# An attention and two-layer feed-forward kernel: fills for TensorE's early waits, the counts' transfer first, a last round by tile, and a new step order

## The chip, the cores and the metric

The kernel runs on one core of one Trainium2 chip. The metric is the device time of an execution in microseconds (us). Three executions of the kernel before took 528.06, 528.44 and 529.01 us; the median is 528.44.

## The reference

All values are 32-bit on the chip (inputs may come as 64-bit words). For 2 batches of 768 tokens, with 8 heads of 64:

```
scores = q k^T / 8, plus -slope(head) * distance; kept where the key is one of the
         first n_global, or among the n_local up to the query's own
x      = softmax(scores) v                          (1536 tokens x 512)
h      = x w_in (512 x 1024);  y = layernorm(h * softmax(h)) * g;  x2 = y w_out (1024 x 512)
g2     = prelu(x2 w_in2, alpha)  (512 x 2048);      out = g2 w_out2 (2048 x 512)
```

## The kernel before, in words

**Tiles.** The 1536 tokens are 12 tiles of 128. For tile i the first stage does: scores (`s{i}`, two steps of eight products, L653), bias and maximum on VectorE (`ttr`, L674), exponentials on ScalarE (`exp`, L686), sums (`sum`, L697), normalising on GpSimd (`norm`, L704), transposes on TensorE into the two `pt` buffers (`pp`, L711), their copies (`ptc`), products with v (`xp`, L732), and a split of the result into a high and a low part (`xh`, `xl`). Then four projection steps (`hp{i}.0` to `hp{i}.3`, L767), each of six 512-wide products with `w_in`, the softmax and normalisation of h, transposes (`yt`, L833), and, for each pair of tiles, the product with `w_out` (`f`, L868). Every large product is made of three: high by high, high by low, low by high.

**Weights.** They arrive as 64-bit words. VectorE decodes a 512-wide unit in three passes (L909, L915, L922), ScalarE casts the high part (L941) and GpSimd subtracts it for the low part (L947). `w_in` has eight units, `w_out` eight. A projection step `hp{i}.c` needs units 2c and 2c+1.

**Second layer.** From about 240 us on, for each batch and each of 16 slices f of the 2048 columns: two products `h` (L1004), the prelu on VectorE, ScalarE and GpSimd (`p`, `q`, `gh`, `gl`), and six steps `o{b}.{f}.{t}`, one for each of six tiles t, that add slice f into tile t's accumulator (L1046). After f = 15 each tile is copied out of the accumulator (`ev`) and stored (`out`); the very last tile goes in two halves.

**Who sets the order.** All of this is a list of steps (`p.op`) with costs, needs, buffers and a due time: a base for each tile plus constants in `PRI` plus a table `ADJ` by step and tile. `Plan.order` (L135) walks it with a cost model: it takes the engine and step that can start first, and among those that can start at once the one with the smallest due time; TensorE stays with its kind of step (fp32r products, transposes, attention products, scores) if one is due within `window`. The steps are then written out by hand in that order; each engine runs its own in order. Three rules of the model matter here. A step's result is ready `DRAIN` + `LAT` after its end, which is 0.22 + 0.05 us behind a TensorE step. TensorE's costs double for 3.5 us after the start and after an idle time of over 2 us. And 30 filler steps (`warm`, L1096) of two transposes of the identity each have due time 1000 and up, so that they go where nothing else can start at once: 15 write the projection's accumulator, 15, after `s2.0`, the accumulator of `xp`.

**Ahead of the plan.** The counts n_global and n_local are loaded on SyncE's queue (L1312); VectorE makes distances from them and a flag that says whether the fast plan applies; every engine loads the flag into a register (L1341) and branches (L1348). Loads written ahead of the branch: the first `w_in` unit on ScalarE's queue (L1320), tile 0's two halves of queries and keys on SyncE's (L1323), two small vectors on ScalarE's, and four more `w_in` units on SyncE's (L1346), written behind the flag's load. What stands outside the plan is ordered by the framework.

```
            if e == "PE":
                if s - free[e] > 2.0:
                    cold = s + 3.5
...
                if s < cold:
                    c *= 2
...
            for j in succ[k]:
                need[j] -= 1
                ready_at[j] = max(ready_at[j], end + (self.LAT if e != "Z" else 0.0))
```

Of the kernel before, what the change touches and what calls it, by code (L numbers as in the profile page):

```python
# [16 lines left out]
P = 128  # L17
B, H, S, D = 2, 8, 768, 64
# [19 lines left out]
    "fb": [12.1, 25.5, -36.9, 15.6, -51.3, -38.9], "window": 40.6, "warm": 30,  # L38
# [10 lines left out]
    "bias": [-14.38, -0.57, -13.62, -36.09, -9.24, 3.17, 79.56, 27.81],  # L49
    "biaso": [-35.88, -34.51, 29.02, -45.8, 12.27, 5.79, 12.9, -39.68],  # L50
    "biase": [11.25, -16.84, -13.23, -15.82, -6.36, -33.05, -25.07, 2.78],
    "lv": [-1.11, -35.58, -25.57, -93.69, -40.77, -64.76, -5.42, -4.44, 16.09, 40.62, 15.31, -13.09],
    "s": [76.17, 48.99, -1.79, -6.29, 18.91, -35.34, -3.19, 1.82, 4.29, 5.11, 37.66, -32.16],
    "ttr": [17.97, 14.68, 9.26, -0.75, 24.27, 1.35, -15.44, 44.7, 38.08, 44.52, 77.23, 18.58],
    "exp": [99.95, 17.84, 75.5, 70.15, 68.93, 21.61, 105.36, 54, 36.83, 49.25, 25.14, 20.37],
    "sum": [65.68, 7.88, 17.67, -22.02, 14.99, 23.4, 68.37, 13.75, 33.79, 44.17, 14.09, 30.57],
    "norm": [-28.87, -32.62, 6.09, -65.61, -51.55, -113.76, -7.63, -51.34, -8.17, -14.02, -57.42, -42.13],
    "pp": [42, 3.18, 9.24, 15.23, 22.4, -52.81, -19.62, 8.44, -19.69, 7.5, -63.78, -27.87],
    "ptc": [31.98, 24.29, 16.59, 13.26, -19.88, 27.62, 55.76, 15.29, 29.15, 39.13, 56.39, 31.43],
# [4 lines left out]
    "wild": [-16.78, -71.31, -22.06, -78.1, -76.78, -74.65, -91.3, -78.16],  # L64
    "wi": [5.84, -7.23, 8.63, 14.11, 39.89, 27.88, 6.37, 30.66],
    "wold": [3.18, -27.83, 0.2, -42.59, -4.05, -51.23, -59.18, -139.63],
# [9 lines left out]
    "wld": [-60.46, 30.51, -6.9, -43.59, -6, -39.28, -71.17, -74.53, -40.67, -27, -26.6, -59.42, -94.56,  # L76
        -71.11, -58.44, -37.12],
    "w": [-6.92, -18.15, -3.62, -19.12, 7.9, -25.84, -46.69, -31.5, 17.04, -9.48, -0.07, 24.34, 23.84, 37.97,
        26.01, 29.91],
    "xsh": [-36.5, -104.9, -69.33, 0.49],  # L80
    "xsl": [-18.31, 12.23, 178.41, 14.34],
    "h": [-0.45, -22.06, -6.71, -25.99, -26.69, -13.38, -21.23, -5.88, -9.22, -36, 7.14, -11.38, -44.05,
        -19.53, -8.32, 9.67, -1.41, -20.25, -27.94, -26.27, -8.77, 13.58, -6.42, -6.67, 5.95, -8.6, 7.18, 4.35,
        -5.24, -5.24, 6.81, -23.86],
    "pre": [47, 15.26, 20.19, 1.09, 5.66, 4.51, 1.73, -56.3, -1.61, -12.93, -24.13, -2.19, -11.64, -7.5,
        -12.94, -11.02, 15.1, -13.05, 1.61, -12.3, -8.69, -9.72, -27.94, -3.94, -30.83, -32.43, -3.34, -7.57,
        -38.89, -39.41, -24.55, -18],
    "o": [25.13, 15.32, 1.71, 16.18, 13.48, 5.18, 9.35, -10.38, 23.35, 48.62, 54.94, 17.03, 51.65, 48.18,
        61.52, 65.49, 53.89, 52.56, 42.95, 51.04, 74.74, 72.62, 64.17, 78.16, 98.8, 63.21, 109.55, 136.07,
        93.51, 111.81, 113.4, 98.74],  # L90
# [10 lines left out]


class Plan:


    LAT = 0.05
    SWITCH = {"r": 0.03, "tr": 0.07, "xp": 0.11, "sp": 0.12}
    DRAIN = {"PE": 0.22, "DVE": 0.09, "ACT": 0.1, "POOL": 0.05}

    def __init__(self, window=2.5):  # L110
        self.ops, self.by_name, self.size = [], {}, {}
        self.window = window

# [21 lines left out]
    def order(self, free):  # L135
# [37 lines left out]
        while done < n:  # L173
# [26 lines left out]
            if e == "PE":  # L200
                if s - free[e] > 2.0:
                    cold = s + 3.5
# [3 lines left out]
                if s < cold:  # L206
                    c *= 2
# [1224 lines left out]
```

## Time and profile before

| what | value |
|---|---|
| median of three executions | 528.44 us |
| the profiled execution: its own time | 528.57 us |
| its span, first to last instruction | 526.8 us |
| TensorE (PE) busy | 504.1 us, 96% |
| VectorE (DVE) busy | 312.5 us, 59% |
| ScalarE (ACT) busy | 202.0 us, 38% |
| GpSimd (POOL) busy | 200.1 us, 38% |
| mean granted clock of TensorE | 0.985 |

The profile is one execution. Times count from the first instruction. PE is TensorE's products (a transpose is one of them), PEld its weight loads, SP is SyncE; a q behind an engine is its sequencer or its DMA queue. L and a number is a line of the kernel. A busy engine may be a slow one: the granted clock of TensorE is given in tenths in the page's slices (forty of 13.2 us each) and as a share in a table of stretches.

### The profile page before, as it was taken

How to read it: one execution, taken by the hardware profiler on the slowest of the kernel's cores; microseconds unless marked ns; L12 is line 12 of the kernel's file. 1: busy time of each engine (PE TensorE's matmuls, PEld its weight loads, DVE VectorE, ACT ScalarE, POOL GpSimd, SP SyncE). 2: the span in 40 equal slices, each digit the busy share in tenths (PEclk: the TensorE clock that was granted, in tenths of full speed). 3: DMA queues.
4: the chain of work that ended last, by engine and by line, in shares of the span. 5: the costliest groups of instructions: out<-in, count | busy, mean ns of one | idle time of the engine just before them, and what ended most of it. 6: DMA issues, size and time to landing. Idle time of an engine off the chain costs nothing.

```text
span 526.8 us, 8161 instructions
## 1 busy us (share of the span) xinstructions
PE 504.1 (96%) x3084; PEld 439.4 (83%) x3084; DVE 312.5 (59%) x671; ACT 202.0 (38%) x488; POOL 200.1 (38%) x205
## 2 busy tenths in 40 slices
PE   3599999999999999999999999999999999999995
PEld 3366778888889789899998998999888899889884
DVE  4979898374443658549976878988622423213130
ACT  4757875374354687334223222232311201101112
POOL 2667776023030338023316566554611412213230
PEclk9779999999999999999999999999999999999999
DMA  6965563132130210202333234340002100000003
GB/s 207 369 216 169 171 212 119 51 100 72 31 101 2 70 42 1 81 0 82 116 125 105 96 119 121 119 126 35 1 1 81 40 1 1 1 0 1 0 2 126
DMA packets 14959, 43.61 MB, mean 83 GB/s; under 512 B 1984, under 2 KB 3264, under 8 KB 14912
## 3 DMA queue, kind: packets, MB, share of 16 engines
q1 hardware_dynamic: 14336, 42.34, 25.3%
q10 hardware_dynamic: 576, 0.67, 0.5%
q8 instruction: 26, 0.43, 0.3%
q14 instruction: 21, 0.17, 0.1%
HBM read 39.86 MB, written 3.15 MB: 82 GB/s over the span
## 4 chain that ended last, share of the span: by engine, by line
PE 90%; DVE 4%; ACT 2%; DMA 1%; issue 1%; POOL 1%; POOLq 0%; DVEq 0%; ACTq 0%
PE m L774 12%; PE m L502 9%; PE m L503 9%; PE m L504 9%; PE h L503 9%; PE h L504 9%; PE h L502 8%; PE x L737 4%; PE s L659 4%; PE pt L716 4%; PE pt L503 3%; PE pt L504 3%; PE pt L502 3%; PE pt L838 2%; PE x L503 1%; PE x L504 1%
## 5 line engine op out<-in xcount | busy, mean ns | idle before, releaser
L1040 POOL TENSOR_TENSOR gl<-t,gh 128x384 fp32r<-128x384 f32 x64 | 70.7, 1107 | 129.5 <-ACT gh L1033 126.5
L1020 DVE TENSOR_SCALAR t<-h,a_sb 128x384 f32<-128x384 f32 x64 | 39.4, 616 | 96.6 <-POOL gl L1040 64.6
L1033 ACT CAST gh<-t 128x384 fp32r<-128x384 f32 x64 | 32.6, 513 | 144.0 <-PE pt L503 77.1
L502 PE MATMUL h<-x2h,w2h 128*128 128x384 f32 x192 | 64.5, 336 | 0.0
L503 PE MATMUL h<-x2l,w2h 128*128 128x384 f32 x192 | 64.5, 336 | 0.0
L504 PE MATMUL h<-x2h,w2l 128*128 128x384 f32 x192 | 64.5, 336 | 0.0
L704 POOL TENSOR_TENSOR pr<-pr,sm 128x512 f32<-128x512 f32 (+1 forms) x48 | 47.3, 1012 | 32.6 <-DVE sm L698 23.4
L502 PE MATMUL m<-lh,woh 128*128 128x256 f32 x192 | 55.8, 290 | 0.0
L503 PE MATMUL m<-ll,woh 128*128 128x256 f32 x192 | 54.2, 282 | 0.0
L504 PE MATMUL m<-lh,wol 128*128 128x256 f32 x192 | 54.2, 282 | 0.0
L686 ACT ACTIVATE pr<-lg,nmx 128x256 f32<-128x256 f32 (+1 forms) x96 | 46.4, 486 | 10.8 <-DVE nmx L674 10.7
L502 PEld LDWEIGHTS m<-lh,woh 128*128 128x128 f32 x192 | 36.4, 190 | 3.8 <-issue 1.5
L947 POOL TENSOR_TENSOR w2l<-wf,w2h 128x512 fp32r<-128x512 f32 x21 | 29.2, 1392 | 26.5 <-ACT w2h L941 26.5
L503 PEld LDWEIGHTS m<-ll,woh 128*128 128x128 f32 x192 | 36.6, 190 | 1.2
L502 PEld LDWEIGHTS h<-x2h,w2h 128*128 128x128 f32 x192 | 36.1, 188 | 1.8
L503 PEld LDWEIGHTS h<-x2l,w2h 128*128 128x128 f32 x192 | 36.0, 188 | 1.8
L816 POOL TENSOR_TENSOR st<-st,mhalf 128x1 f32<-128x1 f32 x12 | 6.6, 549 | 80.7 <-DVE st L811 80.6
L915 DVE SCALAR_TENSOR_TENSOR wf<-wr,wf 128x512 int32<-128x512 int32 x32 | 36.8, 1149 | 0.4
L504 PEld LDWEIGHTS m<-lh,wol 128*128 128x128 f32 x192 | 36.6, 191 | 0.0
L1027 DVE SCALAR_TENSOR_TENSOR t<-h,t 128x384 f32<-128x384 f32 x64 | 35.4, 553 | 1.2
L504 PEld LDWEIGHTS h<-x2h,w2l 128*128 128x128 f32 x192 | 36.0, 188 | 0.0
L774 PE MATMUL m<-wih,xh 128*128 128x512 f32 x96 | 33.6, 431 | 0.7 <-ACT xh L748 0.7
(160 smaller groups left out, 1159.1 us busy)
## 6 DMA issues: line engine op xcount, KB each, us to landing
wr<-in_w_out SPq DMA_DIRECT2D x24, 512.0 KB, 3.6
wr<-in_w_in SPq DMA_DIRECT2D x16, 512.0 KB, 3.5
qk<-in_kq SPq DMA_DIRECT2D x20, 384.0 KB, 4.1
v<-in_vw SPq DMA_DIRECT2D x10, 512.0 KB, 3.7
x<-in_w_in SPq DMA_DIRECT2D x7, 512.0 KB, 6.9
out<-x SPq DMA_DIRECT2D x11, 256.0 KB, 2.1
x<-in_w_in ACTq DMA_DIRECT2D x1, 512.0 KB, 6.3
wr<-in_kq SPq DMA_DIRECT2D x2, 256.0 KB, 6.9
```

The source lines that it names most:

```text
L502: nc.tensor.matmul(o, sh, mh, start=first, stop=False)
L503: nc.tensor.matmul(o, sh, ml, start=False, stop=False)
L504: nc.tensor.matmul(o, sl, mh, start=False, stop=last)
L686: nc.scalar.activation(pr[:, j, :n], self.tiles["lg", i, h][:, :n], AF.Exp, bias=self.tiles["nmx", i, hf][:, hl : hl + 1], scale=-1.0, acc ...
L704: nc.gpsimd.tensor_tensor(pr[:, :, :n], pr[:, :, :n], r.unsqueeze(2).to_broadcast([P, 2, n]), ALU.mult)
L774: nc.tensor.matmul(hp[:, ns], st[:, c, :], mv[:, c, ns], start=f, stop=l)
L915: nc.vector.scalar_tensor_tensor(m["m"], self.tiles["wraw", name][:, :, 1], -0x40000000, m["m"], ALU.bitwise_and, ALU.bitwise_or)
L947: self.eng(e).tensor_tensor(lo, src(), f32(hi), ALU.subtract)
L1020: nc.vector.tensor_scalar(t, o(), 0.0, self.a_sb[:, f : f + 1], ALU.min, ALU.mult)
L1027: nc.vector.scalar_tensor_tensor(t, o(), 0.0, t, ALU.max, ALU.add)
L1033: nc.scalar.copy(gh, self.tiles["t", b, f, n])
L1040: nc.gpsimd.tensor_tensor(gl, self.tiles["t", b, f, n], f32(self.tiles["gh", b, f, n]), ALU.subtract)
```

## The change

- The 30 `warm` steps go. Instead, ahead of a scores, `pp`, `xp`, `yt` or first projection step, `idle()` writes as many transposes of the identity as the planner's own idle time before that step holds: (idle - 0.2) / 0.11, for steps that start before 60 us of its clock and waits over 0.35 us. Until the first projection step is placed they write the projection's accumulator; after it, the step's own output, and then only the wait after that output is free is counted.
- 24 transposes of the identity are written ahead of the branch, behind the flag's load.
- The first `w_in` unit is loaded on SyncE's queue behind the first half of tile 0's queries and keys; beside the counts' transfer only the two small ones are issued first.
- In the model a TensorE step may follow a TensorE step that it needs at once, and costs no longer double.
- In the last batch a tile's step for f = 14 waits for the tile before to have had f = 15.
- Some buffer releases and first uses name all tiles instead of the last one or two.
- `window` and every number of `ADJ` are new (cut here).

```diff
@@ -35,7 +35,7 @@
 YN_ACT = 1
 PRI = {
     "hpb": [-22.7, -30.5, -41.3, -50.8, -5.7, 15.7, -32.6, 6.6, 14.8, -15.7, -2.9, 22.1],
-    "fb": [12.1, 25.5, -36.9, 15.6, -51.3, -38.9], "window": 40.6, "warm": 30,
+    "fb": [12.1, 25.5, -36.9, 15.6, -51.3, -38.9], "window": 119.5, "warm": 30,
     "base": [-80.5, -35.1, -9.2, -5.2, 15.5, 19.1, 66.6, 102.8, 108.9, 162.8, 180.8, 178.6], "bias0": 11.1,
     "biaso": 4.0, "biase": 39.9, "load": 13.1, "s": 13.0, "sum": -26.6, "norm": 50.1, "pp": -26.4,
     "ptc": -0.2, "xp": -4.8, "xh": -42.6, "hp": -3.1, "ln": 30.3, "yt": 46.9, "f": 45.8, "x2c": 55.8,
@@ -46,48 +46,47 @@
 }
 START = {"PE": 6.0, "DVE": 6.2, "ACT": 6.1, "POOL": 6.45, "SP": 6.1, "Z": 6.0, "DMA": 14.0}
 ADJ = {
...
 }
 SCALE = 0.125
 
@@ -104,6 +103,7 @@
 
 
     LAT = 0.05
+    FILL = 60.0
     SWITCH = {"r": 0.03, "tr": 0.07, "xp": 0.11, "sp": 0.12}
     DRAIN = {"PE": 0.22, "DVE": 0.09, "ACT": 0.1, "POOL": 0.05}
 
@@ -154,7 +154,9 @@
         free = dict(free)
         dma = free.pop("DMA", 0.0)
         cand = {k for k in range(n) if need[k] == 0}
-        done, last, res, shared, cold = 0, None, [], 0.0, free["PE"] + 3.5
+        done, last, res, shared = 0, None, [], 0.0
+        self.fill = {}
+        res_hp = [None]
 
         def slot_time(o):
             r = 0.0
@@ -198,13 +200,15 @@
             o = ops[k]
             cand.discard(k)
             if e == "PE":
-                if s - free[e] > 2.0:
-                    cold = s + 3.5
+                early = res_hp[0] is None
+                idle = s - (free[e] if early else max(free[e], slot_time(o)))
+                if o[0].startswith("hp"):
+                    res_hp[0] = s
+                if s < self.FILL and idle > 0.35:
+                    self.fill[o[0]] = int((idle - 0.2) / 0.11), early
                 if o[6] != last and last is not None:
                     s += self.SWITCH[o[6]] + 0.2 * (last == "sp")
                 last = o[6]
-                if s < cold:
-                    c *= 2
             if o[9] and e == "DVE":
                 c += max(0.0, free["POOL"] - s)
                 shared = s + c
@@ -229,7 +233,8 @@
                     released[u[0]][place[u]] = freed[u]
             for j in succ[k]:
                 need[j] -= 1
-                ready_at[j] = max(ready_at[j], end + (self.LAT if e != "Z" else 0.0))
+                same = e == "PE" and "PE" in ops[j][1]
+                ready_at[j] = max(ready_at[j], free[e] if same else end + (self.LAT if e != "Z" else 0.0))
                 if need[j] == 0:
                     cand.add(j)
             res.append((s, free[e], e, k))
@@ -593,6 +598,12 @@
             else:
                 nc.vector.tensor_copy(dst, xp[:, : 2 * P])
 
+    def idle(self, o):
+
+        count, early = self.fill
+        for _ in range(count):
+            self.nc.tensor.transpose(self.hp[:, :P] if early else o, self.ident, self.ident)
+
     def eng(self, e):
         return {"DVE": self.nc.vector, "ACT": self.nc.scalar, "POOL": self.nc.gpsimd}[e]
 
@@ -653,6 +664,7 @@
         for hf in range(2):
             rawslot = ("raw", (i, hf)) if i else ("wr", ("r", hf))
             def emit(e, hf=hf):
+                self.idle(self.sq[0][:, :P])
                 for j in range(2):
                     for pj in range(2):
                         w = self.tiles["qk", i, hf][pj * D : (pj + 1) * D, j]
@@ -711,6 +723,7 @@
             def emit(e, pair=pair):
                 pr = self.tiles["pr", i, pair]
                 pp = self.tiles["pp", i, pair] = self.next_pt()
+                self.idle(pp[:, :P])
                 for j in range(2):
                     for c in range(nch):
                         nc.tensor.transpose(
@@ -731,6 +744,7 @@
 
             def emit(e, pair=pair):
                 pt, vs = self.tiles["pt", i, pair], self.vs[i]
+                self.idle(self.xp[:, pair * P : (pair + 1) * P])
                 for c in range(nch):
                     for j in range(2):
                         h = pair * 2 + j
@@ -766,6 +780,8 @@
         for c in range(NC):
             def emit(e, c=c):
                 xh, xl = self.tiles["xh", i], self.tiles["xl", i]
+                if c == 0:
+                    self.idle(hp[:, :P])
                 for st, mv, f, l in (
                     (xh, self.wih, c == 0, False), (xh, self.wil, False, False), (xl, self.wih, False, c == NC - 1)
                 ):
@@ -833,6 +849,7 @@
         for q in range(2):
             def emit(e, q=q):
                 pp = self.tiles["yt", i, q] = self.next_pt()
+                self.idle(pp[:, :P])
                 for c in range(4):
                     f = q * 4 + c
                     nc.tensor.transpose(pp[:, c * P : (c + 1) * P], y()[:, f * P : (f + 1) * P], self.ident)
@@ -994,8 +1011,8 @@
                     p.op(f"xsl{b}.{n}.{c}", None, {"DVE": 0.5, "POOL": 1.03}, b0 + PRI["xs"] + 0.1 * c, emit, port=True,
                          after=[f"xsh{b}.{n}.{c}"], uses=[(f"x2s{n}", b)])
             accs = [self.hp[:, 0:512], self.hp[:, 512:1024], *self.pts, self.xp, self.m2]
-            ln = f"{self.last}"
-            first = [[f"sq{ln}"], [f"sq{ln}"], ["cl_pt"], ["cl_pt"], [f"xl{ln}"], [f"xc{self.last_pair}.{NC - 1}"]]
+            sq, xl, xc = ([f"{s}{i}{x}" for i in range(k)] for s, x, k in (("sq", "", 12), ("xl", "", 12), ("xc", ".3", 6)))
+            first = [sq, sq, ["cl_pt"], ["cl_pt"], xl, xc]
             for f in range(NF2):
                 fb = b0 + f * PRI["m2f"]
                 for n in range(2):
@@ -1052,6 +1069,8 @@
                     dep = [f"gl{b}.{f}.{t // 3}", f"w{f}.1lo", f"o{b}.{f - 1}.{t}"]
                     if f == 0:
                         dep += first[t] if b == 0 else []
+                    if b == B - 1 and f == NF2 - 2 and t > 0:
+                        dep.append(f"o{b}.{NF2 - 1}.{t - 1}")
                     g = ("gh", (b, f, t // 3)), ("gl", (b, f, t // 3))
                     pri = fb + PRI["o"] + (0.5 * t if not tail else 3 * t - (NF2 - 1 - f) * PRI["m2f"] + 8)
                     p.op(f"o{b}.{f}.{t}", "PE", 0.69, pri, emit, after=dep, uses=[(f"acc{t}", b), *g], kind="r")
@@ -1093,15 +1112,6 @@
         self.plan_bias(p, ats)
         for i in range(n):
             self.plan_attn(p, i, r0, ats, at)
-        for k in range(PRI["warm"]):
-            early = k < PRI["warm"] // 2
-
-            def emit(e, o=self.hp if early else self.xp):
-                for c in range(2):
-                    nc.tensor.transpose(o[:, c * P : (c + 1) * P], self.ident, self.ident)
-
-            p.op(f"warm{k}", "PE", 0.22, 1000.0 + k, emit, kind="tr", after=[] if early else ["s2.0"],
-                 uses=[] if early else [("x", f"warm{k}")])
         units = [(c, h) for c in range(NC) for h in range(DF // DM)]
         for u, (c, h) in enumerate(units):
             cs = slice(h * DM, (h + 1) * DM)
@@ -1141,11 +1151,11 @@
             self.open_pool("hp2", pools, space=bass.MemoryType.PSUM)
             pools["hps"] = [pools["hp2"].tile([P, 512], F32, name=f"h2{k}") for k in range(2)]
 
-        p.op("cl_s", "Z", 0.0, 0, close_s, after=[f"ttr{last}.{h}" for h in range(H)])
-        p.op("cl_ats", "Z", 0.0, 0, close(["ats"], "m2", "w2c"), after=[f"exp{i}.{h}" for i in seq[-2:] for h in range(H)])
+        p.op("cl_s", "Z", 0.0, 0, close_s, after=[f"ttr{i}.{h}" for i in seq for h in range(H)])
+        p.op("cl_ats", "Z", 0.0, 0, close(["ats"], "m2", "w2c"), after=[f"exp{i}.{h}" for i in seq for h in range(H)])
         p.op("cl_at", "Z", 0.0, 0, close(["at"], "w2a"), after=["cl_ats", f"hp{last}.{NC - 1}"])
         p.op("cl_wo", "Z", 0.0, 0, close(["wo", "m1"], "w2b"), after=["cl_at", f"f{self.last_pair}.{NC - 1}.1"])
-        p.op("cl_pt", "Z", 0.0, 0, None, after=[f"ll{last}.{q}" for q in range(2)])
+        p.op("cl_pt", "Z", 0.0, 0, None, after=[f"ll{i}.{q}" for i in seq for q in range(2)])
         self.plan_moe2(p, pools)
         return p
 
@@ -1176,6 +1186,7 @@
         with self.tc.manual_schedule():
             for name, e, emit in p.order(START):
                 if emit is not None:
+                    self.fill = p.fill.get(name, (0, False))
                     emit(e)
         for name in ("w2b", "w2a", "w2c", "m2", "hp2"):
             self.pool_cms.pop(name).__exit__(None, None, None)
@@ -1317,10 +1328,11 @@
     em.w_in_alloc(cpool)
     r0 = []
     wl = []
-    wl.append(em.w_in_raw[0](nc.scalar.dma_start))
     for hf in range(2):
         r = wring.tile([P, 2 * DM], F32, "wr", "r0")
         r0.append(em.load_raw(0, hf, r))
+        if hf == 0:
+            wl.append(em.w_in_raw[0]())
     nc.scalar.dma_start(em.g_sb, em.g_ln)
     nc.scalar.dma_start(em.a_sb, em.alpha)
     with tc.high_priority():
@@ -1343,8 +1355,11 @@
     ps = ctx.enter_context(tc.tile_pool(name="ps", bufs=1, space=bass.MemoryType.PSUM))
     em.psum_pools(ps)
 
+    wm = em.ps_m1("wm")[:, :P]
     while len(wl) < len(wring.bufs["wx"]):
         wl.append(em.w_in_raw[len(wl)]())
+    for _ in range(24):
+        nc.tensor.transpose(wm, em.ident, em.ident)
     with tc.If(rv > 0) as cmp:
         em.fast_phase(wring, nw, r0, wl)
     with cmp.Else():
```

## Rows read from the trace of the kernel before

**Rows 1.** The page: busy time of the engines, the clock by slices, the chain's shares.

```profile
PE 504.1 (96%) x3084; PEld 439.4 (83%) x3084; DVE 312.5 (59%) x671; ACT 202.0 (38%) x488; POOL 200.1 (38%) x205
...
PEclk9779999999999999999999999999999999999999
...
PE 90%; DVE 4%; ACT 2%; DMA 1%; issue 1%; POOL 1%; POOLq 0%; DVEq 0%; ACTq 0%
```

**Rows 2.** Stretches: length, busy us by engine, granted clock, DMA share, GB/s.

```profile
8.40:34.40 26.00, 19.04 (x98) 14.25 (x98) 23.13 (x69) 17.78 (x61) 11.90 (x15) 0.74 0.86 308
...
19.60:24.00 4.40, 1.38 (x5) 0.50 1.02 411
...
34.40:80.00 45.60, 44.30 (x331) 32.38 (x330) 41.36 (x117) 35.89 (x94) 35.07 (x34) 1.00 0.60 185
...
520.30:526.80 6.50, 1.08 (x8) 0.85 (x8) 0.42 (x1) 0.37 (x1) 0.00 (x0) 0.85 0.55 185
34.40:520.30 485.90, 483.93 (x2980) 424.30 (x2979) 286.97 (x593) 182.31 (x424) 185.95 (x171) 1.00 0.22 68
```

**Rows 3.** The chain, steps at the full clock: start, us, engine, tile, line.

```profile
41.44 1.02 PE x L737 x16
...
44.07 1.06 PE s L659 x8
45.13 1.60 PE m L774 x6
...
82.31 1.39 PE m L774 x6
...
90.20 0.87 PE pt L716 x8
```

**Rows 4.** TensorE's waits: who for whom, us in total, times, longest.

```profile
PE s L659 <- DMA qk<-in_kq: 3.2, 1, 3.2
```

**Rows 5.** The chain's first transfer; SyncE's queue in the timeline, 5 to 9.3 us.

```profile
0.74 5.53 DMA ni<-in_n
...
8.38 1.29 SPq L445 DMA_DIRECT2D x<-in_w_in  x3
```

**Rows 6.** DMA issues of the last stores: KB each, us from issue to landing.

```profile
out<-x SPq DMA_DIRECT2D x1, 256.0 KB, 2.0
...
out<-x ACTq DMA_DIRECT2D x1, 128.0 KB, 4.6
```

**Rows 7.** The fillers' line in three stretches: ns min/median/max, first and last start; a stretch.

```profile
L1101 PE MATMUL m<-ident x6: 421/421/421, 10.2 to 11.3; 128*128 128x128 f32 x6
...
L1101 PE MATMUL m<-ident x11: 272/273/273, 13.2 to 14.3; 128*128 128x128 f32 x11
...
60.00:300.00 240.00, 1.58 (x10) 1.18 (x10) 1.00 0.27 80
```

**Rows 8.** The chain, 24 to 29.3 us; then VectorE in the timeline, idle time in brackets.

```profile
24.04 1.08 PE pt L716 x4
25.13 1.48 PE x L737 x12
26.61 2.01 PE s L659 x8
28.62 0.65 PE x L737 x4
...
28.76 0.42 DVE L674 CUSTOM_DVE_ANT_0 lg<-s,biaso 128x256 f32<-128x256 f32 x1 [1.47 <-PE s L659]
...
35.60 0.42 DVE L674 CUSTOM_DVE_ANT_0 lg<-s,biase 128x256 f32<-128x256 f32 x1 [1.11 <-PE s L659]
```

**Rows 9.** VectorE by line, 8 to 26 us: the second of a unit's three passes.

```profile
L915 DVE SCALAR_TENSOR_TENSOR m<-x,m 128x512 int32<-128x512 int32 x6 | 4.1, 690 | 0.0
```

**Rows 10.** The end: a stretch, and the last activations on GpSimd.

```profile
519.00:523.00 4.00, 2.38 (x14) 1.60 (x12) 0.42 (x1) 1.52 (x3) 0.00 (x0) 1.00 0.99 361
...
512.58 1.01 POOL L1040 TENSOR_TENSOR gl<-t,gh 128x384 fp32r<-128x384 f32 x1 [1.04 <-ACT gh L1033]
```

More of the change, by code (lines that the diff above doesn't have):

```diff
@@ L48 @@
 ADJ = {
[L49 to L59, printed above, removed]
[4 rows of a table removed]
-    "wild": [-16.78, -71.31, -22.06, -78.1, -76.78, -74.65, -91.3, -78.16],
@@ L65 @@
-    "wi": [5.84, -7.23, 8.63, 14.11, 39.89, 27.88, 6.37, 30.66],
-    "wold": [3.18, -27.83, 0.2, -42.59, -4.05, -51.23, -59.18, -139.63],
[9 rows of a table removed]
[L76 to L87, printed above, removed]
@@ L88 @@
-    "o": [25.13, 15.32, 1.71, 16.18, 13.48, 5.18, 9.35, -10.38, 23.35, 48.62, 54.94, 17.03, 51.65, 48.18,
-        61.52, 65.49, 53.89, 52.56, 42.95, 51.04, 74.74, 72.62, 64.17, 78.16, 98.8, 63.21, 109.55, 136.07,
-        93.51, 111.81, 113.4, 98.74],
+    "bias": [-15, 218.7, 220.4, 84.5, 30.2, 251.7, 462.2, 330.9],
+    "biaso": [69.1, -90.2, 98.2, -102.4, -52.3, 100.5, 205.3, 34.2],
+    "biase": [-256.7, -21.5, -21.5, 46.2, 14, 198.7, -71.8, 154.5],
+    "lv": [146.5, 31.6, -130.7, 105.3, 137.9, -212.2, -21.3, 57.1, 203.2, 112.7, 85.4, 30.9],
@@ new lines @@
+    "s": [256.9, 191.8, -103.6, 381.8, 156.7, -1.6, 28.3, 175.1, 148.7, 195.7, 150.9, -64.4],
+    "ttr": [136.5, -100.5, -256.8, -133.5, -27.5, -86.1, -120, 228.4, 93.8, 96.6, 195.2, 81.6],
+    "exp": [278.1, 153.5, -17.3, 174.1, 303, 117.2, 50.2, 225.6, 271, 53.2, -229.9, -71.8],
+    "sum": [62.8, 208, -84, 95.5, 286.5, -62.6, 248.2, 211.2, 228.9, 236.7, 25.9, 142.7],
+    "norm": [4.9, -1.9, -132.9, -34.2, -55.5, -333.8, 17.9, -253.3, -218.8, 9.6, -362.3, -451],
+    "pp": [80.5, -12.1, 12.6, 116.2, 413, 88.1, 33.3, 99, 177.2, 57.5, -215, 9.2],
@@ new lines @@
+    "ptc": [57.9, 63.5, 28.9, 224.8, 86.9, 45.3, -27.7, 214.6, 163.5, 137.5, 74.9, 178.8],
[4 rows of a table added]
+    "wild": [216.3, 52.5, -35.2, -73, 76, 86, -15.4, 364.6],
+    "wi": [101.8, 49.2, 81.8, 32.1, 265.5, 65.2, 99.6, 272.1],
+    "wold": [194.8, -15.5, -69.2, -24, -319.6, 242.6, -120.9, -418.7],
[9 rows of a table added]
+    "wld": [-194.8, 19.5, -45.8, -49, -16.1, 52.7, -255.2, -112.5, -57.5, -0.2, 47.5, -85.2, -125, -89.4, 51.3,
+        -179.2],
+    "w": [-92.5, 29, 7, 109.9, 239.2, -34.6, 28, 70.2, 203.5, 191.5, 159.9, 375.9, 223, 253, 230.1, 433.6],
@@ new lines @@
+    "xsh": [-120, -7.6, -301.3, 292.2],
+    "xsl": [225.2, 219.5, 905, 128.9],
+    "h": [131.8, 295.5, 173.7, 161.8, 99.7, 254, 205.4, 240.3, 143.8, 174.2, 340.3, 154.3, 204.1, 204, 304.7,
+        274, 247.5, 133.2, 214.8, 172.9, 111.5, 222.8, 244.1, 132.7, 210.9, 154.6, 205, 293.6, 203.3, 178.7,
+        312.8, 205.2],
+    "pre": [-69.4, -77.4, -102.6, -41.7, -133.8, -86.8, -165.3, -230.1, -156.4, -178.2, -200.3, -145.8, -126,
+        -116.7, -193.6, -173.2, -50.6, -229.7, -281.8, -285.5, -242.4, -122.5, -178.1, -125.3, -315.4, -172.9,
+        -199.9, -221.3, -284.5, -257.7, -200.8, -227.6],
@@ L91 @@
+    "o": [1.6, -51.6, 31.9, 68.6, 46.2, -52.7, 8.2, 6.6, 126.8, 142.7, 204, 49.5, 168.4, 189.3, 200.1, 220.5,
+        144.1, 115.4, 238.1, 225.8, 170.6, 168.3, 121.2, 175, 263.8, 152.3, 129.9, 337, 147.9, 323.3, 215.7,
+        153.9],
 }
```

26 rows, old and new, of the table ADJ are left out of this document.

## The prediction, made before the result was known

> **What bounds the kernel now.** I read the page first: TensorE is busy 96% of the span and is 90% of the chain that ended last [rows 1]. So a change pays only where TensorE idles, runs slowly, or does work that isn't needed. The clock digits are low in the second and third slice alone [rows 1]. Then I cut the span by stage [rows 2]. From 34.4 to 520.3 us TensorE is busy 483.9 of 485.9 us: that stretch has 2.0 us to give, plus whatever is removed from it. [...] Before 8.4 us TensorE does nothing, and after 520.3 nothing that the output needs; the span ends 6.5 us later.
>
> How much of the 26.0 us up to 34.4 is needed? At the full clock the work done there would take: scores of tile 1, 2 x 1.06, and of tile 0, half as wide, some 2 x 0.6; eight transposes 0.87; sixteen attention products 1.02; two of tile 0's four projection steps 2 x 1.39 [rows 3]. Sum 8.0. So the start wastes 18.0 us on top of the first 8.4. These, the 6.5 us at the end, the 2.0 us of idle time and the dummies already there are all that can be had; the rest, some 490 us, is work.
>
> What holds the start? The longest wait of TensorE behind the first scores is 3.2 us, for tile 1's queries [rows 4]. In front of them stands the transfer of the two counts, 0.74 to 6.27 us, from which VectorE works out the flag; the flag also holds SyncE, whose next three weight loads go out only at 8.38 [rows 5]. VectorE itself is busy 23.1 of the 26.0 us, and 41.4 of the next 45.6 [rows 2]: it is nearly the bound of the start.
>
> **The change, part by part.** The sum is made against the profiled execution: its own time 528.57, of which 526.8 is the span; the 1.8 us around it stay. The median, 528.44, is 0.13 below.
>
> *Counts first.* A 512 KB load that went out together with the counts moves from ScalarE's queue to SyncE's, behind the first half of tile 0's queries. The counts (2 KB) took 5.5 us [rows 5]; a 256 KB store with nothing beside it took 2.0 [rows 6]. The gain lies between 0 and 3.5; I take 1.7, the middle, as other loads still follow at once. It moves flag, branch, bias tables and the held loads alike. The moved load comes 256 KB later in its queue, some 0.7 us at the 361 GB/s of a full stretch [rows 10]; the bias tables give VectorE work until then.
>
> *Warm clock.* The 30 transposes behind the first scores and the 30 spread later go; 24 stand ahead of the branch, and each wait that the planner sees in the first 60 us of its own clock is filled. Do such transposes raise the clock? In the trace they do: six starts from 10.2 to 11.3 us, 421 ns each, then eleven from 13.2 to 14.3, 273 ns each, with only their like between [rows 7]. After the 3.2 us wait the granted clock is 0.50 [rows 2, 4]. On the chain from 24.0 to 29.3, four transposes, twelve products, scores and four products take 1.08 + 1.48 + 2.01 + 0.65 = 5.2 us [rows 8]; at the full clock 2.6. That is what TensorE gains; VectorE is late next. Its idle time there that TensorE caused is 1.47 + 1.11 = 2.6 us [rows 8]. Bounds: 0, if VectorE's work just moves; 5, if the projection steps up to 32.7 us, at the same clock, gain their half too. I take 3.0, near the idle time.
>
> [...]
>
> *Order.* All step priorities are new, and the planner no longer doubles costs while it thinks the clock cold, nor adds 0.27 us between a TensorE step and a TensorE step that needs it. What order results I can't read off the table. Bounds: the terms above take 4.7 of the 18.0 us; of the 13.3 left, VectorE's decoding of eight weight units, three passes of 0.69 us each [rows 9], 16.6 us in all before tile 0's projection is through, allows perhaps half, 6.6; below, a worse order could lose 4. I take 3.0. The second edit also lets steps of one kind follow each other. A projection step behind scores takes 1.60 us, between its like 1.39 [rows 3]: a change of kind costs 0.1 to 0.2. I count 128 such changes between 34.4 and 245 us. A quarter fewer would bring 4; the new table could also add some. I take 1.0 (-1 to 4).
>
> *Dummies removed later.* Of the 30 late ones ten stand in 60 to 300 us [rows 7], as many in 30 to 60, and two in 300 to 520: 22 x 0.11 = 2.4 us. Some filled waits that stay; I take 1.5 (0 to 2.4). The other eight run after the last output product and cost nothing. The new fills cost nothing where the wait is as long as planned, since 0.2 us of it is left open. Behind an overrun stand the real step and then VectorE, which waits for its scores; I count that with the stalls below.
>
> *Last f by tile.* Now the last two f go round one after the other, so tiles finish 0.69 us apart and six stores crowd: 519 to 523 us has a DMA share of 0.99, and the last half store takes 4.6 us to land instead of 2.0 [rows 6, 10]. Then tile t's last two steps follow each other: tiles finish 1.37 us apart, and 256 KB need 0.7 us at 361 GB/s. The crowd is gone; the last landing should take 2.0 to 2.6 us. Gain 0 (if something else delays the last one) to 2.6; I take 2.2. Tiles 3 to 5 need the last activations, ready at 513.6 [rows 10]; they come three pairs, 4.1 us, behind 512.0: no wait.
>
> *New stalls.* An in-order TensorE in a denser start will meet waits that the planner missed; the like in the trace is the 2.0 us after 34.4. I take -1.5 (0 to -4).
>
> Sum: 1.7 + 3.0 + 3.0 + 1.0 + 1.5 + 2.2 - 1.5 = 10.9. 528.57 - 10.9 = 517.7; against the median, 517.5.
>
> **The rivals.**
> (1) *The dummies don't hold the clock: slower.* Then each costs 0.21 us, as from 10.2 to 11.3, and not the 0.11 [rows 7] with which their count is computed. The start has up to 18 us of waiting, room for about 150; 150 x 0.10 = 15 us of overrun ahead of the real steps, and the 3.0 are gone: -10.9 + 3.0 + 15 = +7.1, 535.7. It decides from some 80 dummies at the lower clock ((10.9 - 3.0) / 0.10). [...] Against it: rows 7. Chance 0.07.
> (2) *VectorE becomes the bound of the start.* It is busy 89 to 91% up to 80 us [rows 2]; a faster TensorE then waits for decoded weights. Clock and order bring 1.0 instead of 6.0, and the stalls are in it: 1.7 + 1.0 + 1.0 + 1.5 + 2.2 = 7.4, 521.2. Against it: ScalarE has 8.2 us free up to 34.4 [rows 2] and may take some copies and bias tables. Chance 0.25.
> (3) *The 24 don't do what they say.* In the text the flag's load into registers stands ahead of them; if they run behind it, they push the first scores by up to 24 x 0.21 = 5.0 us: 522.7. For it: three of the four weight loads written behind the flag's load ran behind it [rows 5]. Against it: one did not, and TensorE has nothing else to do. Chance 0.09.
> (4) *The order is worth much more*: 6.6 in the start and 4 for changes of kind: 517.7 - 6.6 = 511.1. Chance 0.11.
>
> **How the numbers follow.** The forecast has 0.48, in a range of its own of 513 to 521. The predicted time is 517.5. With 521.2, 522.7 and 511.1 and some spread about each, 509 to 526 leaves out rival 1 and about 0.1 at the two ends. Within 0.2% (1.1 us) is about what a measurement can't tell from no change. Every case but the first is faster by more; of the forecast some 0.05 loses its order as well (-4 for +3, stalls -4 for -1.5: 527 and above) and lies near the old time or over it. So faster 0.88, same 0.03, slower 0.09.
>
> **What would show it.** Counts: VectorE's first instruction near 4.6 us instead of 6.3, first scores near 6.7. Clock: 1.00 in every stretch from the first scores on; scores of tile 1 in about 1.1 us a half. Order: tile 0's first projection step near 22 us and its last done by 36, not 46.7. Tail: 4.3 us from the last product to the end. Changes of kind: fewer than 128. I am wrong if the clock shows 0.50 after the branch, if a wait of several us stands on TensorE after 34 us, or if the loss of the start only moves from TensorE's clock to waits on VectorE.

## The result, and the profile after

The changed kernel takes 519.63 us (median of four runs, 519.20 to 520.03); the kernel before, beside it, 528.30 (528.06 to 529.01). The ratio is 0.9832, 95% interval [0.9816, 0.9848]: 8.7 us by the medians. Forecast: 517.5 in 509 to 526. The profiled execution took 519.2 us with a span of 517.4, against 528.57 and 526.8: 9.4 us less span.

The page of the changed kernel: busy times, and the granted clock by slice.

```profile
PE 507.8 (98%) x3183; PEld 447.5 (86%) x3183; DVE 309.2 (60%) x667; ACT 204.0 (39%) x490; POOL 202.0 (39%) x207
...
PEclk9999999999999999999999999999999999999999
```

The low digits of the second and third slice [rows 1] are gone. TensorE is busier in a shorter span because dummies, 159 in place of 60, count as busy. Two stretches of the changed kernel, the first cut as in [rows 2], the second up to its last product: length, then busy time of each engine (instructions), granted clock, DMA share.

```profile
8.40:34.40 26.00, 24.10 (x199) 19.86 (x197) 24.55 (x70) 17.19 (x58) 15.04 (x15) 1.00 0.92 335
34.40:512.80 478.40, 476.75 (x2940) 420.98 (x2938) 279.89 (x578) 182.45 (x423) 184.24 (x170) 1.00 0.22 69
```

VectorE went from 23.1 to 24.55 us busy of the 26 us between 8.4 and 34.4: almost no room is left there. Behind 34.4 us TensorE idles 478.40 - 476.75 = 1.65 us. TensorE's three largest waits over the whole span (total, times, longest), where [rows 4] stood before:

```profile
PE pt L729 <- POOL pr L716: 1.8, 4, 0.7
PE wm L1362 <- POOL warm L292: 1.5, 1, 1.5
PE s L671 <- DVE nmx L686: 0.9, 1, 0.9
```

The start on TensorE, in time order (start, duration, count; in brackets the idle time before it and its releaser). L1362 are the 24, L605 the fills, L671 scores, L790 projection:

```profile
1.46 4.53 PE L1362 MATMUL wm<-ident 128*128 128x128 f32 x24 [1.46 <-POOL warm L292]
5.91 0.72 PE L671 MATMUL s<-wr 64*128 64x128 f32 x8
6.56 5.68 PE L605 MATMUL m<-ident 128*128 128x128 f32 x50
13.11 0.71 PE L671 MATMUL s<-wr 64*128 64x128 f32 x8 [0.87 <-DVE nmx L686]
13.75 5.02 PE L605 MATMUL m<-ident 128*128 128x128 f32 x44
18.70 1.13 PE L671 MATMUL s<-qk 64*128 64x256 f32 x8
...
23.86 2.95 PE L605 MATMUL m<-ident 128*128 128x128 f32 x25
26.56 0.71 PE L790 MATMUL m<-wih,xh 128*128 128x512 f32 x2
...
36.50 0.73 PE L790 MATMUL m<-wih,xh 128*128 128x512 f32 x2
```

The first projection step of the kernel before:

```profile
29.93 1.22 PE L774 MATMUL m<-wih,xh 128*128 128x512 f32 x2 [0.69 <-ACT xh L748]
```

The real steps run at the full rate from 5.91 us on: scores of tile 0 take 0.72 and 0.71 us, of tile 1 1.13 and 1.14; in the kernel before the slowest of them took 1.23 and 2.08. But the 44 fills end and scores follow with no wait in brackets: that fill was longer than the wait that it filled. The first projection step stands at 26.56 us; it was at 29.93. The third, at 36.50, is a mark for what follows: from its start to the end of the last product the changed kernel takes 476.26 us, and all the kernels with its order below take 476.25 to 476.34, so what a part is worth in the start can be read there. Two pieces of the chain that ended last:

```profile
0.74 2.79 DMA ni<-in_n
...
13.82 4.95 PE m L605 x44
```

The counts took 2.79 us, 5.53 in [rows 5]. The chain runs through the 44 fills, but not through the 25 ahead of the projection: from 20.24 to 34.84 us it lies on ScalarE and VectorE. The last product:

```profile
512.37 0.39 PE L509 MATMUL m<-w2h,gl 128*128 128x512 f32 x1
```

From the end of the last product, 512.76, to 517.4 are 4.6 us; they were 6.5 [rows 2].

### The profile page after: what moved, and what is told of

It reads as the page before. It is cut to its first block, busy times and chain, and to the rows that moved or that the text cites. A ratio compares the mean times of both kernels' runs of the same rounds, so it can differ in the third digit from the quotient of the medians.

```text
span 517.4 us, 8357 instructions
## 1 busy us (share of the span) xinstructions
PE 507.8 (98%) x3183; PEld 447.5 (86%) x3183; DVE 309.2 (60%) x667; ACT 204.0 (39%) x490; POOL 202.0 (39%) x207
## 4 chain that ended last, share of the span: by engine, by line
PE 88%; DVE 6%; ACT 2%; DMA 1%; POOL 1%; issue 1%; SPq 0%; DVEq 0%; ACTq 0%; POOLq 0%
PE m L790 11%; PE m L507 9%; PE m L509 9%; PE m L508 9%; PE h L507 9%; PE h L509 9%; PE h L508 8%; PE x L751 3%; PE s L671 3%; PE pt L729 3%; PE pt L508 3%; PE pt L509 3%; PE pt L507 3%; PE pt L855 2%; PE x L509 1%; PE x L508 1%
## 5 line engine op out<-in xcount | busy, mean ns | idle before, releaser
L964 POOL TENSOR_TENSOR w2l<-wf,w2h 128x512 fp32r<-128x512 f32 x20 | 27.2, 1360 | 27.7 <-ACT w2h L958 26.4
L939 DVE SCALAR_TENSOR_TENSOR wf<-wr,wf 128x512 int32<-128x512 int32 x32 | 33.3, 1042 | 0.6
L964 POOL TENSOR_TENSOR wil<-wf,wih 128x512 fp32r<-128x512 f32 x14 | 18.0, 1289 | 37.2 <-ACT wih L958 37.2
L932 DVE SCALAR_TENSOR_TENSOR wf<-wr,wf 128x512 int32<-128x512 int32 x32 | 31.5, 984 | 0.4
```

The source lines that it names most:

```text
L939: nc.vector.scalar_tensor_tensor(m["w"], self.tiles["wraw", name][:, :, 0], 29, m["m"], ALU.logical_shift_right, ALU.bitwise_or)
L964: self.eng(e).tensor_tensor(lo, src(), f32(hi), ALU.subtract)
```

## The experiments

Each run's time is a median, each ratio is to the kernel before beside it; the changed kernel stands at 0.9832.

### Taking parts back from the changed kernel

**No dummies.**

```diff
-    for _ in range(24):
-        nc.tensor.transpose(wm, em.ident, em.ident)
...
-        for _ in range(count):
+        for _ in range(0):
```

> The changed kernel, same order of steps, without any filler transpose: none of the 24 ahead of the branch, none of the 135 in the waits. Theory 1 (the clock counts): the granted clock falls to 0.50 in the waits of 13 to 25 us, the steps up to about 30 us take twice as long, and the 3.0 us of the prediction's clock term come back: 522.6 against 519.6 for the changed kernel. Theory 2 (VectorE bounds the start): the clock falls too, but VectorE, busy 24.6 of the 26 us from 8.4 to 34.4, hides the slower steps: at most 0.8 us, 520.4 or less.

Measured 521.32, 0.9865 [0.9849, 0.9882]: 1.7 us slower than with them, between the two theories. Its start:

```profile
5.70 1.23 PE L671 MATMUL s<-wr 64*128 64x128 f32 x8 [5.70 <-DVE dist L340]
...
16.79 2.08 PE L671 MATMUL s<-qk 64*128 64x256 f32 x8 [2.44 <-DMA qk<-in_kq]
...
26.73 0.73 PE L790 MATMUL m<-wih,xh 128*128 128x512 f32 x2 [1.43 <-ACT xh L762]
...
37.87 0.73 PE L790 MATMUL m<-wih,xh 128*128 128x512 f32 x2
```

Scores took 2.08 us at 16.79 us, where a half of tile 1 takes 1.13 in the changed kernel, and the next ones, from 23.25 on, still 1.68; yet the projection begins at 26.73, only 0.17 later than with dummies, since s1 starts 1.9 us sooner, at 16.79. The price shows in the steps behind it: the transposes at 30.11 us in the changed kernel stand at 31.47, and the third projection step, at 37.87, is 1.37 late.

**Fills, but not the 24.**

```diff
-    for _ in range(24):
-        nc.tensor.transpose(wm, em.ident, em.ident)
```

> The changed kernel with the 135 fills but without the 24 transposes ahead of the branch. Theory 1: the first scores run at the lower clock (8 products in about 1.2 us instead of 0.65), the 50 fills behind them start at the lower clock and overrun by about 2 us, which hits the second half of tile 0's scores: 521. Theory 2: VectorE releases that half only at 13.1 us, 0.9 us after the fills ended, so an overrun of 2 us delays it by about 1.1 us and VectorE has other work meanwhile: 519.6 to 520.2.

521.29, 0.9865 [0.9848, 0.9881], as without any dummy, and near the 521 of theory 1. The first scores take 1.23 us and the 50 fills 7.06 in place of 5.68: without the 24 the fills themselves are slower, by 1.38 us in all, and all behind them is about 0.73 late. The profiled run, 520.11, is the fastest of the four by 1.0 us; what the other three lost beyond it, no trace shows.

**Counts late again.**

```diff
+    wl.append(em.w_in_raw[0](nc.scalar.dma_start))
     for hf in range(2):
...
-        if hf == 0:
-            wl.append(em.w_in_raw[0]())
```

> The changed kernel with the first w_in unit loaded on ScalarE's queue ahead of everything, as before. VectorE's first instruction goes back from 3.55 to about 6.3 us, the first scores from 5.9 to about 8.5. Theory 1 (the start is a chain from the counts): the 2.7 us come back in full, 522.3. Theory 2 (the transfers, near saturated from 5 to 28 us, set the pace of the decoding): half of it or less, 521.0 or below.

522.69, 0.9893 [0.9876, 0.9909]: 3.1 us lost, more than the 2.7 of theory 1. Its start:

```profile
8.41 0.71 PE L671 MATMUL s<-wr 64*128 64x128 f32 x8 [1.60 <-DVE dist L340]
9.05 5.68 PE L605 MATMUL m<-ident 128*128 128x128 f32 x50
14.66 0.71 PE L671 MATMUL s<-wr 64*128 64x128 f32 x8
15.31 5.02 PE L605 MATMUL m<-ident 128*128 128x128 f32 x44
20.26 1.13 PE L671 MATMUL s<-qk 64*128 64x256 f32 x8
...
28.12 0.71 PE L790 MATMUL m<-wih,xh 128*128 128x512 f32 x2
...
38.06 0.73 PE L790 MATMUL m<-wih,xh 128*128 128x512 f32 x2
```

Between scores and projection no wait is left at all: a fixed number of dummies follows, however late they start. 28.12 - 8.41 = 19.71 us. The third projection step is 1.56 late. The rest of the loss isn't in the start: the profiled run, 521.71, is the fastest of the four, and its end, 5.5 us from the last product, is 0.9 longer with the same last round.

**Last f as before.**

```diff
-                    if b == B - 1 and f == NF2 - 2 and t > 0:
-                        dep.append(f"o{b}.{NF2 - 1}.{t - 1}")
+                    if b == B - 1 and f == NF2 - 1:
+                        dep.append(f"o{b}.{NF2 - 2}.{NT - 1}")
```

> The changed kernel with the last two f one round after the other (all six tiles of f = 14, then all six of f = 15), as before. Theory (crowded stores): from the last product to the end 6.5 us instead of 4.6, so 521.5. Rival (the last store is slow by itself): no difference, 519.6.

520.79, 0.9854 [0.9838, 0.9871]: 1.2 us, below the 1.9 expected. The last product ends at 512.90 and the span 6.0 us later, against 4.6. But that distance isn't a fixed one: in the kernels here that have the new last round it lies between 4.6 and 5.5 us, and without it, as here or in the old order, between 6.0 and 6.5.

**The order alone**: no dummies, counts late, and no condition on the last f. The diffs of the runs without dummies and with late counts together, and of the one on the last f the two lines that go; nothing is put in their place. So, unlike what the expectation says, the last round is not that of before: in the trace three tiles are copied out from 508.68 us on and the other three only from 512.76 on, and from the last product, at 514.08, to the end are 5.6 us.

> The changed kernel with its order written out as it is, but the counts last as before, none of the dummy transposes (neither the 24 nor the fills) and the last f after all of the one before it as before: the one thing left of the change is the order (the table, and the conditions and the delay that it was found with) and that the old 60 dummies are gone. Theory 1 (the parts add up): 519.6 plus what each part cost when it alone was taken back, 3.1 for the counts, 1.7 for the dummies and 1.1 for the tail, is 525.5; so the order is worth 528.05 - 525.5 = 2.5 us, near the 3.0 (with the changes of kind 4.0) of the prediction. Theory 2 (the order earns nothing by itself, it only lets the earlier start be used): within 0.5 us of the kernel before without its dummies, 527.5 to 528.5. Theory 3 (the parts overlap: a later start hides the dummies' loss, as VectorE is late in any case): 523.5 to 524.5.

521.7, 0.9887 [0.9866, 0.9908]; its five runs stand in two groups, three at 521.5 to 521.7 and two at 523.8 and 524.05. Against the kernel before without its dummies (below) that is 6.3 us by the medians, 5.7 by the ratios: none of the three theories was near enough, though the third had the direction. Some 0.5 of it stands at the end (6.1 us from the last product there, 5.6 here). What the three parts cost when each was taken back alone, 3.1 + 1.7 + 1.2 = 6.0, came to 2.1 (by the ratios 2.9) when all went. Part of that is the last round, which here was not taken back whole. The rest shows in the start:

```profile
8.80 1.22 PE L671 MATMUL s<-wr 64*128 64x128 f32 x8 [8.80 <-DVE dist L340]
...
18.71 2.08 PE L671 MATMUL s<-qk 64*128 64x256 f32 x8 [2.79 <-DVE m L926]
...
26.65 0.73 PE L790 MATMUL m<-wih,xh 128*128 128x512 f32 x2 [1.42 <-ACT xh L762]
...
37.80 0.74 PE L790 MATMUL m<-wih,xh 128*128 128x512 f32 x2
```

First scores 3.1 us later than without dummies alone (5.70), and the projection at the same place, 26.65 against 26.73. Without dummies late counts are absorbed in waits. The start of the third projection step in the four kernels, in us:

| | counts first | counts late |
|---|---|---|
| with the 24 and the fills | 36.50 | 38.06 |
| without dummies | 37.87 | 37.80 |

Each part is worth 1.4 to 1.6 us only where the other is in place; the two together are worth 1.3. This doesn't hang on the last round; it is one profiled run of each kernel.

**The changed kernel with the table of before.**

```diff
-    "fb": [12.1, 25.5, -36.9, 15.6, -51.3, -38.9], "window": 119.5, "warm": 30,
+    "fb": [12.1, 25.5, -36.9, 15.6, -51.3, -38.9], "window": 40.6, "warm": 30,
...
```

Every number of `ADJ` is the old one too.

> The changed kernel with the step priorities and the window of before: all other parts of the change stay, the two edits of the planner's model too. The order has 122 changes of kind on TensorE, against 125 in the changed kernel and 143 before. Theory 1 (the model's edits and the parts do it): 519.6 to 520.5. Theory 2 (the new priorities carry the order's part): the 3 us of the prediction's order term come back, 522.6.

543.3, 1.0276 [1.0254, 1.0298]: slower than both kernels and outside both theories. The start is as good (first projection step at 26.76 us); the loss comes later. The stretch from 160 to 240 us, then the largest wait of TensorE over the span:

```profile
160.00:240.00 80.00, 70.75 (x537) 60.22 (x537) 44.79 (x99) 36.67 (x88) 20.93 (x20) 1.00 0.10 27
```

```profile
PE s L672 <- DVE nmx L687: 4.0, 3, 2.9
```

In the changed kernel TensorE is busy for all 80.00 of these. So what the prediction called the order is not a table plus a model whose gains add: the table fits one model. The new table with the old model was not run, so what each brings by itself stays open.

### Putting parts on the kernel before

**Its 60 dummies left out, same order.**

```diff
-                if emit is not None:
+                if emit is not None and not name.startswith("warm"):
```

> The kernel before, same order of steps, without its 60 filler transposes. Theory (the late fillers cost): 22 of them between 30 and 520 us at 0.11 us each, less what filled waits, 1.5 us: 526.8 against 528.3. Rival (they stand in waits or in VectorE's shadow): 528.3, no difference.

528.05, 0.9994 [0.9985, 1.0003]: no difference that can be told. Taken together, the old dummies neither helped nor cost; the late ones alone were not taken out.

**Old order, with the 24 and fills where its model sees waits** (44, 45, 3, 16, 11, 1).

```diff
...
+                    if s < 60.0 and idle > 0.35:
+                        self.fill[o[0]] = int((idle - 0.2) / 0.11), not seen_hp
...
+    for _ in range(24):
+        nc.tensor.transpose(wm, em.ident, em.ident)
```

> The kernel before, same order of steps, its 60 fillers replaced by 24 ahead of the branch and by fills in the waits of its own plan, counted as in the change. Theory 1 (the clock counts by itself): TensorE runs at the full clock from the first scores on, and beside the 1.5 us of the removed fillers some 3 us of the start come through: 523.8. Theory 2 (the order was made for the slow clock, VectorE bounds it): beside the 1.5 us at most 1: 525.8 to 526.8.

The old 60 are left out here too. 527.53, 0.9982 [0.9971, 0.9993]: 1.0 us (thirteen runs, 526.85 to 531.67), less than either theory had; some 0.6 of it, by the ratios, goes beyond leaving the 60 out. The 24 are over at 5.9 us there, scores start only at 8.75, and in the profiled run, the longest of the thirteen, they take 1.23 us again, after 2.89 us of waiting.

**Counts first alone.** The edit of the change.

> The kernel before with only the counts' transfer first (the first w_in unit on SyncE's queue behind tile 0's first half). Theory 1 (the start is a chain from the counts): first scores at 5.9 instead of 8.4 us and the end 2.4 to 2.9 us earlier, as taking it out of the changed kernel cost: 525.6. Theory 2 (in the old order tile 1's queries and the clock come later in the chain and swallow it): 527.3 or more.

526.84, 0.9967 [0.9954, 0.998]: 1.7 us, the figure of the prediction, between the two theories. The first projection step stands at 28.57, where it was at 29.93.

Alone on the kernel before, the counts and the fills (without the old dummies) give 1.7 + 1.0 = 2.7 us; they were not tried together there.

### Further on from the changed kernel

**A shorter fill ahead of s1** (24 in place of 44).

```diff
+                    if name.startswith("s1."):
+                        self.fill = min(self.fill[0], 24), self.fill[1]
```

> The changed kernel with at most 24 dummy transposes ahead of each half of s1.0 and s1.1, where it has 44 ahead of s1.0: they ran 13.75 to 18.77 us, and without dummies s1.0 could begin at 16.79, when its keys landed. Theory 1 (VectorE, busy 24.55 of 26 us, sets the pace of the start): s1.0 is 2 us earlier, hp0.0 stays at 26.5 to 26.7, time within 0.4 of 519.6. Theory 2 (the overlong fill holds the start back): hp0.0 and what follows 1 to 2 us earlier, 518.0 to 518.6.

519.37, 0.9823 [0.9809, 0.9836]: inside theory 1's band. The first scores of tile 1 start at 16.55, 2.2 us sooner, but the transposes behind them then wait 1.3 us for GpSimd, and the projection gains 0.34.

**Weight loads ahead of the flag.**

```diff
+    while len(wl) < len(wring.bufs["wx"]):
+        wl.append(em.w_in_raw[len(wl)]())
     nc.scalar.dma_start(em.g_sb, em.g_ln)
...
-    while len(wl) < len(wring.bufs["wx"]):
-        wl.append(em.w_in_raw[len(wl)]())
```

> The changed kernel with the four loads of the tensor in_w_in that stand behind the flag on SyncE written ahead of the flag's load. Theory 1 (the flag holds them until 5.64 us, and VectorE then waits 0.45 us at 10.2 us for the first of them, and VectorE sets the pace): they go out at 4.6 to 5.2 us, VectorE's decodes up to 30 us each start 0.4 to 0.6 earlier, hp0.2 near 36.0 in place of 36.5: 518.8 to 519.4. Theory 2 (the queue is full anyway, its transfers share one width): the keys of s1 land later by as much and nothing is gained, 519.4 to 519.9. Slower, over 520, if the earlier loads delay the 512 KB that the first scores read or the counts behind it.

519.5, 0.9821 [0.9808, 0.9835]: not told apart from the changed kernel. The second decode of VectorE starts at 9.71 in place of 10.23; the first scores start at 6.50, behind the 24, which took 5.12 us in this run, and from there to the projection at 26.20 are 19.70 us, the same fixed distance as with late counts.

**Both, and a shorter fill ahead of the projection** (at most 20 ahead of tile 1's scores, 12 ahead of the projection; the diff without the early loads).

```diff
+                    cap = {"s1.": 20, "hp": 12}
+                    for key, most in cap.items():
+                        if name.startswith(key):
+                            self.fill = min(self.fill[0], most), self.fill[1]
```

> The changed kernel with the four early loads written ahead of the flag's load and shorter fills: at most 20 dummies ahead of each half of s1, at most 12 ahead of a tile's first projection step (it has 44 and 25). The chain that the fills make is then shorter by 24 + 13 dummies of 0.114 us, 4.2 us in all. Theory 1 (the fixed number of dummies holds the start: in the kernel with the counts late the steps were late by as much as the first scores, in the one without dummies they were not): hp0.0 near 25.0 to 25.5 in place of 26.56, and the time 518.0 to 518.7. Theory 2 (behind the dummies VectorE and GpSimd are as late, as in the two runs with one of these edits, where 0.35 us at hp0.0 were lost again to waits on GpSimd's pr): hp0.0 25.0 to 25.5 too, but the waits on pr and xl grow by what it gains, 518.9 to 519.6. Over 520 if TensorE's clock falls in the gaps that are left.

518.56 (518.31 to 519.08), 0.9811 [0.9797, 0.9824]: the lowest of all, about 1.1 us below the changed kernel by the ratios; the intervals overlap by 0.0008, so it isn't settled. Its start, and its largest wait over the span:

```profile
24.76 0.72 PE L790 MATMUL m<-wih,xh 128*128 128x512 f32 x2
...
26.43 0.73 PE L790 MATMUL m<-wih,xl 128*128 128x512 f32 x2 [0.47 <-DVE xl L769]
...
35.90 0.73 PE L790 MATMUL m<-wih,xh 128*128 128x512 f32 x2
```

```profile
PE pt L729 <- POOL pr L716: 3.6, 5, 1.4
```

The projection begins 1.8 us sooner (24.76); a third of that is left at the third projection step (35.90, where the changed kernel has 36.50). The rest went into waits on GpSimd, 3.6 us in place of 1.8, and on VectorE's xl, 0.5. Both theories hold in part. Here, then, the projection began 2.0 us before the 26.73 us that it has without dummies.

## Why the prediction was right, and where its steps were not

The time lay 2.1 us from the forecast, and the chances were on the right side. That the sum came so near is in part luck: the order brought about 2 us more than its terms and the stalls cost 1.5 less, while the counts and the clock together, the late dummies and the last round brought less. By the ratios the gain, 8.9 us, is 5.7 for the order, 2.9 for counts, dummies and last round together, and 0.3 for leaving out the old dummies. Term by term:

- *Counts first*, 1.7: 1.7 on the kernel before, 3.1 in the changed one (1.56 of it at the third projection step), nothing that a trace shows in the start without dummies. VectorE's first instruction moved to 3.55 us (4.6 forecast), the first scores to 5.91 (6.7).
- *Warm clock*, 3.0: 1.7 in the changed kernel, 1.0 on the kernel before. The clock itself came as forecast: 1.00, scores of tile 1 in 1.13 us a half. Two steps failed. "The new fills cost nothing where the wait is as long as planned" didn't apply: the wait ahead of tile 1's scores was shorter, so that they could start at 16.79 and started at 18.70. That was the smaller part, for cutting this fill brought only 0.34 us at the third projection step. The larger is that the 3.0 were set near the whole idle time that TensorE caused on VectorE, and 1.4 to 1.7 came through. That VectorE had other work in line there is what the chain above speaks for; no run tries it by itself.
- *Order and changes of kind*, 3.0 + 1.0: 5.7 to 6.3, some 0.5 of it at the end; the term that was sized too low. The two kernels without dummies have the same products; their busy lines, the kernel before first, then the order alone:

```profile
PE 495.6 (94%) x3024; PEld 431.2 (82%) x3024; DVE 312.1 (59%) x671; ACT 202.0 (38%) x488; POOL 200.2 (38%) x205
```

```profile
PE 492.5 (95%) x3024; PEld 431.1 (83%) x3024; DVE 307.9 (59%) x667; ACT 203.7 (39%) x490; POOL 201.7 (39%) x207
```

Fewer by 3.1 us busy for the same 3024, up to the last product 2.6 us less idle (24.2 against 21.6), and some 0.5 at the end: the 6.1 between the spans, but for rounding. Over the program TensorE changes its kind of step 118 times where it changed 137 times (103 times for 128 in the stretch that the prediction counted); at the 0.1 to 0.2 us of the prediction 19 fewer are 2 to 4 us. Counted kind by kind, 1.4 of the 3.1 us lie in the first 184 products (the first 40 scores, 40 transposes, 56 attention products and 48 of the projection), up to some 60 us, where equal steps run at different rates too (the second half of tile 1's scores takes 1.89 us in the one, 1.13 in the other), and 1.8 behind them; from 36.8 to 511 us the granted clock is 1.00 in both. Together this is a little less than that estimate. Why the new order waits 2.6 us less, no run separates.

- The forecast of *where* the order would help was wrong: tile 0's first projection step came at 26.56, not 22, and its last began at 41.67, not by 36. The estimate took half of the start's waste to be free; VectorE, 24.55 of 26 us busy, had no such half. The order alone moved that first step from 29.96 to 26.65, 3.3 us.
- *Dummies removed later*, 1.5: taking all 60 out changed 0.3 to 0.5 us, nothing that can be told from none. The 0.11 us of each was also not what [rows 7] show of the late ones, ten of which were 1.58 us busy.
- *Last f by tile*, 2.2: 1.2 by time; the distance from last product to end went from 6.5 to 4.6 (4.3 forecast) in the profiled run, but lies between 4.6 and 5.5 over all kernels that have the new last round.
- *New stalls*, -1.5: none behind 34.4 us, 1.65 of idle against 2.0. The overruns that were counted with them stand in the start.

The terms also don't add. In the changed kernel the fills make TensorE a queue of fixed length in the start: 19.71 and 19.70 us from first scores to projection in two kernels whose scores start 1.9 us apart, and 20.65 in the changed kernel, 0.87 of it waiting. That queue sets the first projection step, but not alone the pace behind it. With the counts late, no fill is on the chain that ended last: from 8.92 to 20.07 us it lies on VectorE, whose work starts 2.7 us later. Without dummies, with the counts first, it lies on TensorE from 19.12 to 24.98 us, most of the way with slower products (eight attention products 1.12 us in place of 0.66, scores 1.68 in place of 1.14). Either way the third projection step comes at 37.8 to 38.1 us. So two bounds lie nearly level there, and taking back the first part is dear, the second cheap.

Of the rivals, (1) fell: fills cost 0.114 us each (5.02 / 44), not 0.21, and the granted clock was 1.00. (3) fell: the 24 ran from 1.46 us, before the flag was known, and held up the first scores by 0.2 us (5.91 against 5.70 without them), by more only in the two runs where they took 5.12 and 5.38 us. Of (2), the bound on VectorE is there, and in part the loss of the start did move to it; the time is not, as order and tail gained elsewhere. (4) had the direction: the order was worth about 2 us more than its terms, not the 6.6 that it asked for. Against rival 1 stand the 24 as well: with nothing before them, they went from 421 ns to 272 ns, and the first scores behind them took 0.72 us in place of 1.23; the group in the changed kernel (shortest, median, longest):

```profile
L1362 PE MATMUL wm<-ident x24: 272/421/476, 1.5 to 5.7; 128*128 128x128 f32 x24
```

## What to carry to other kernels

A fixed count of dummies held up the steps behind it here once a wait had shrunk (19.71 and 19.70 us from first scores to projection, though the scores start 1.9 us apart), so a later improvement of the start should be tried with a recount (here, together with earlier loads, some 1.1 us, not settled). Take parts back singly and all together, and look for a step behind which all variants run alike: here the third projection step showed 1.56 and 1.37 us for two parts taken back singly and 1.30 for both, which means that two bounds lie close together. Priorities found by search belong to the cost model that they were found with; change one alone and tens of microseconds can go (543.3 against 519.6).

## What the runs showed of the hardware

In the kernel without dummies the granted clock of a stretch reads 1.00 where scores took 2.08 us, against 1.13 in the changed kernel:

```profile
16.79:23.20 6.41, 6.15 (x28) 3.42 (x28) 6.24 (x18) 4.09 (x15) 4.83 (x6) 1.00 1.03 408
```

The durations are the safer sign there. When the transposes go from 421 to 272 ns differs from run to run: the 24 took 4.53 us in the changed kernel and 5.35 and 5.38 in two others that write them in the same way (counts late; early loads and shorter fills), the last with not one under 421 ns. Whether that rate is lost in a wait isn't told by the wait's length alone. After 1.60 us (counts late) scores still took 0.71, after 2.89 us (old order with fills) 1.23; but in the kernel before, after 3.21 us, a half of tile 1's scores took 1.13, the time that it takes in the changed kernel, and only from 19.6 us on does the clock read 0.50 [rows 2]:

```profile
18.47 1.13 PE L659 MATMUL s<-qk 64*128 64x256 f32 x8 [3.21 <-DMA qk<-in_kq]
```

And a transfer of 2 KB took 5.53 us when a 512 KB load was issued at the same moment on another queue, and 2.79 when only a 4 KB one was, though 256 and 512 KB followed it on its own queue from 1.19 us on.
